# An attention block fused with a squared-ReLU feed-forward block: six early output tiles as half sums, and loads issued in other places

## The chip, the cores and the metric

The kernel runs on one core of one Trainium2 chip. A core has five engines with queues of their own: TensorE (PE in the profile; its weight loads are PEld), VectorE (DVE), ScalarE (ACT), GpSimd (POOL) and SyncE (SP), and 16 DMA engines that all queues share. The metric is device time in microseconds (us).

## The reference

Attention with a softmax that has one more term in its denominator, over 8 batches of 12 heads, 448 positions and 64 dimensions; its output, as 3584 tokens of 768, goes through two matrix products with a squared ReLU between them.

```python
scores = scale * np.matmul(q, k.transpose(0, 1, 3, 2))
m = np.max(scores, axis=-1, keepdims=True)
e = np.exp(scores - m)
attn = e / (np.sum(e, axis=-1, keepdims=True) + np.exp(-m) + 1e-09)
x = matmul(attn, v), heads side by side            # (3584, 768)
h = x @ w_in                                       # (3584, 2048)
g = np.maximum(h, 0.0) ** 2
out = g @ w_out                                    # (3584, 768), float32
```

The term exp(-m) beside the shifted sum is a 1 beside the unshifted one, so the kernel takes no maximum: it computes exp(scores), sums it, and takes exp(-ln(sum + 1)) as the reciprocal (both sides scaled by 1/256).

## The kernel before, in words

Everything on TensorE is float16 with float32 sums. Heads go in quads of four (`NQ` = 3 quads a batch), keys in chunks of 64 (`KC` = 7). The steps are written out by hand as short words in two strings, and one loop issues them in that order. `ORDER` (L662) covers batches 0 to 2; `CYCLE` (L719) is one period of the software pipeline and runs for batches 3 to 7, each time with that batch's scores, the feed-forward input of the batch before it and the output tiles before that. A tail (L754 to L762) ends the last batch. Every engine takes its instructions in the order of the string and waits for operands by semaphores; so a step that waits holds all later steps of its own engine, and of no other.

The words of `ORDER`, with the engine in brackets:

- `d`: start a load (POOL's DMA queue; the transposing loads and all stores are on SP). The numbers index `LOADS` (L614): 0 to 7 are q and k of one quad of batches 0 to 2, 8 to 13 are v of batches 0 and 1 by quad, 14 is v of batch 2, 15 to 18 are quarters of W_in ("chunks" below), 19 to 22 are quarters of W_out, 23 is `stage(3)`, 24 is `load_third`.
- `W` (PE): matmuls on a constant, to keep the array at work while the first loads come. `c` (ACT or DVE): casts of the first quad.
- `t`, `T` (PE): transposes of q and k into PSUM; `u`, `U` (DVE, or ACT where the last number is 1): their copies to SBUF.
- `s` (PE): scores into one of two double banks `sp`; `e` (ACT): the exponential, which frees that buffer. So a score waits for the exponential of the last but one score. Numbers 0 to 23 are pieces of batch 0, split in two halves of the queries, three quads, and four pieces each: 0 to 3 are quad 0 of the first half, 12 to 15 quad 0 of the second. Numbers from 24 are whole chunks of later quads.
- `p`, `v` (PE): exp(scores) times v. `b`, `a` (DVE): adding the exponentials over chunks; `y`, `S` (PE): the rest of that sum, by ones. `z`, `Z` (ACT): ln(sum + 1); `n`, `M` (ACT): the exponential of minus that; `x`, `X` (DVE): the product with the attention output, which gives `xt`.
- `i`, `j` (PE): `xt` times a block of W_in (`i` is half a batch, two blocks; `j` a whole batch, one block, in pieces). `r`, `k` (ACT or DVE): ReLU; `g`, `l` (DVE): its square, into `gs`.
- `o n,f0,f1` (PE): tile n of the output, 128 tokens by 384 columns, the products with blocks f0 to f1 of `gs`. `O n,act` (ACT or DVE): its way out of PSUM, and its store. `EARLY` = 6 such tiles lie in `ORDER`.
- `P`: PSUM changes hands. Up to there, results other than scores have two banks (`m_psum`) and a double bank; afterwards a ring of four banks (`ring`). A bank is used again by the fourth allocation after, once it has been emptied.

TensorE's 128x128 array can be used whole (128*128 in the profile), in two halves by columns (128*64) or in four quarters (64*64) that work side by side. Scores, products with v and sums use 64*64; transposes use 128*64; `i` and `j` of `ORDER` use 128*128, `j` of `CYCLE` 128*64. `out_piece` (L536) has both ways for output tiles: whole, with one bank; or with `rows` in quarters, where the two halves of the 128 hidden rows sum into two banks `op` and `lo`. In that case `out_first` (L553) takes the first bank out of PSUM, and `out_second` (L561) adds the second on DVE and stores. `ORDER` uses the whole form and `out_done`; `CYCLE` uses quarters and has the word `Q` for `out_second`.

From batch 3 on, q and k come through DRAM: `stage(b)` (POOL queue) writes them as float16, `transposed_loads(b)` (SP) reads them back transposed in three planes of the tile `qk`, `tail_keys(b)` (POOL) copies the last 64 keys of each head, and `load_v_quads(b)` (POOL queue) loads v. In `CYCLE` the word `d0`, near its end, issues all of this for the next batch, and `stage` for the one after.

Of the kernel before, what the change touches and what calls it, by code (L numbers as in the profile page):

```python
# [16 lines left out]
def kernel(  # L17
# [142 lines left out]
    def transposed_loads(b):  # L160
        qk = qks[b] = qk_pool.tile([128, 3, COLS], FP16, name="qk")
        for i, n, x, c in ((0, "q", FRONT, H * S // 2), (1, "k", FRONT, H * S // 2), (2, "k", 0, COLS)):
            nc.sync.dma_start(
                out=qk[:, i, 0:c],
                in_=stages[n, b][x:x + c * 2 * D].rearrange("(r c) -> r c", c=2 * D),
                transpose=True,
            )
# [3 lines left out]
    def tail_keys(b):

        km = kms[b] = flat.tile([128, H, 64], FP16, name="flatq")
        for r in range(2):
            for odd in range(2):
# [445 lines left out]
    def quad_visit(n):  # L621
# [33 lines left out]
        "O": lambda n, act: out_done(128 * (n // 2), HALF * (n % 2), HALF, act),
    }

    def other_ring():
# [8 lines left out]
        U1,0,1,0,7,0 e14 e15 s17 p14 b3,0 b3,1 e17 s18 i0,7 d17 d5 b3,2 e18 b3,3 p15 y3 z3 b4,0 r0,7,0 s21 s19 e21 T1,1,1 d4 n3 b4,1 i0,6 U1,1,1,0,7,0 s20 d15
        T1,1,0 x3 b4,2 e19 b4,3 d16 s23 p16 p17 p18 r0,6,0 U1,1,0,0,7,0 e20 b5,0 e23 s22 e22 b5,1 p19 y4 s26 z4 n4 i0,4 g0,7 x4 r0,4,0 s27 i0,5 g0,6 b5,2 e26
        s25 e27 T1,2,1 s28 e25 p20 p21 r0,5,0 p22 s24 g0,5 b5,3 e28 d11 T1,2,0 p23 e24 s29 y5 e29 U1,2,1,0,7,0 U1,2,0,0,7,0 T2,0,0 T2,0,1 U2,0,0,0,7,0 z5 g0,4
        d6 U2,0,1,0,7,0 s30 n5 s32 a0,0 e30 d13 i0,0 i0,1 s33 x5 e32 r0,0,0 g0,0 r0,1,0 s31 i1,0 d12 g0,1 e33 i0,3 r1,0,0 e31 r0,3,1 s35 d7 s36 e35 P0 e36  # L670
        i0,2 s34 e34 a0,1 a0,2 g1,0 v0,0 a0,3 S0 v0,1 v0,2 v0,3 v0,4 Z0 v0,5 v0,6 M0 r0,2,0 g0,3 g0,2 s37 i1,3 a1,0 a1,1 e37 X0 r1,3,0 a1,2 g1,3 i1,6 s39 s40
        a1,3 e39 i1,1 r1,1,0 r1,6,0 s43 T2,2,0 e40 d20 T2,2,1 g1,6 e43 s42 g1,1 e42 U2,2,0,0,7,0 s41 d19 i1,5 r1,5,0 e41 s38 e38 T2,1,0 T2,1,1 U2,2,1,0,7,0
        U2,1,0,0,7,1 S1 a2,0 Z1 s44 U2,1,1,0,7,0 i1,4 i1,2 a2,1 e44 r1,4,1 s45 a2,2 g1,5 a2,3 v1,0 v1,1 M1 v1,2 v1,3 v1,4 v1,5 v1,6 r1,2,1 v2,0 S2 v2,1 X1
        g1,4 e45 g1,2 v2,2 v2,3 v2,4 Z2 v2,5 v2,6 M2 s47 X2 s46 i1,7 j3,0,2 r1,7,0 o0,0,4 j3,2,4 j1,0,2 j3,4,6 k3,0 j12,0,2 o0,4,8 j1,2,4 o0,8,12 e46 e47
        o0,12,16 s50 d21 g1,7 s51 j12,2,4 j1,4,6 k1,0 j5,0,2 e51 e50 l3 j5,2,4 j5,4,6 d23 O0,1 k5,1 j12,4,6 l5 o1,0,4 s48 s49 j6,0,2 e49 l1 e48 d22 k12,1 l12
        o1,4,8 o1,8,12 o1,12,16 s53 s52 e52 e53 j6,2,4 j10,0,2 o5,0,4 j6,4,6 O1,1 s55 k6,0 s54 j10,2,4 o5,4,8 j0,0,2 e55 a3,0 j10,4,6 j8,0,2 o5,8,12 j0,2,4
        a3,1 k10,1 o5,12,16 e54 s61 s57 l6 a4,0 j14,0,2 O5,0 e57 j14,2,4 j14,4,6 e61 j8,2,4 a3,2 j9,0,2 j9,2,4 j0,4,6 j9,4,6 a3,3 j8,4,6 l10 s56 k0,0 k14,0
        e56 l0 k8,1 s58 o2,0,4 o2,4,8 l14 d14 s59 v4,0 v4,1 v4,2 v4,3 a4,1 v4,4 v4,5 e58 k9,0 s60 e59 s64 o2,8,12 d24 l9 o2,12,16 a4,2 a4,3 j7,0,2 e60 v4,6
# [39 lines left out]

    CYCLE = """  # L719
# [5 lines left out]
        e3,1 o4,2,4 o6,14,16 s3,2 e3,3 o4,4,6 O6,1 a2,2 o4,6,8 s3,5 a2,3 o4,8,10 Q6 o4,10,12 e3,2 e3,5 o4,12,14 o4,14,16 O4,1 Q4 a3,0 s3,6 v2,0 v2,1  # L725
        S2 Z2 v2,2 v2,3 v2,4 v2,5 M2 v2,6 e3,6 X2 j2,0,2 j2,2,4 j2,4,6 k2,0 j13,0,2 j13,2,4 l2 j13,4,6 j3,0,2 k13,1 l13 j3,2,4 j15,0,2 j12,0,2 j15,2,4
        j0,0,2 j3,4,6 a3,1 j15,4,6 k3,1 a3,2 k15,1 j12,2,4 a3,3 l15 j0,2,4 j0,4,6 l3 j12,4,6 j10,0,2 j10,2,4 j4,0,2 k0,0 l0 k12,1 l12 j10,4,6 j6,0,2
        j7,0,2 j7,2,4 j7,4,6 j4,2,4 k10,0 j6,2,4 j4,4,6 l10 j6,4,6 k7,1 j5,0,2 l7 j5,2,4 k4,1 j11,0,2 k6,0 j11,2,4 j11,4,6 j9,0,2 l6 j5,4,6 l4 j9,2,4
# [62 lines left out]
```

## Time and profile before

| | us |
|---|---|
| median of 3 runs | 397.14 (396.34 to 397.28) |
| profiled execution | 396.87 |
| its span | 394.8 |
| PE busy | 385.5 (98%) |
| DVE busy | 240.5 (61%) |
| ACT busy | 238.1 (60%) |
| POOL busy | 59.8 (15%) |

The span is the time from the first to the last instruction; the rest of the execution's time lies around it. Matmuls are pipelined, so the busy time of PE includes their overlap; how fast PE gets on is read from the distance between starts. A row of instructions gives its count after x, then busy us and the mean ns of one, then the idle time of its engine before it and what ended it. The first cycle starts with the first product of values that reads the tile `nn`, at 105.9 us, and the next ones at 151.1, 197.5, 242.8, 288.0; the tail follows at 333.2.

### The profile page before, as it was taken

The page shows a single profiled execution, that of the slowest core. Times are in us where ns is not written, and L with a number is a line of the kernel's source. Part 1 is how long each engine was busy: PE and PEld are TensorE (multiplying, and loading weights), DVE is VectorE, ACT ScalarE, POOL GpSimd, SP SyncE. Part 2 cuts the span into 40 slices and gives each one's busy share as a digit, 9 for nine tenths or more (in the row PEclk, how much of TensorE's full clock was granted, in tenths as well). Part 3 has the DMA queues.
Part 4 walks back from the last instruction along what each step waited for, and adds up shares of the span by engine and source line. Part 5 has one row for each costly group of instructions (what it writes and reads, how often), then busy time and mean ns, then how long its engine had stood idle before and what let it go on. Part 6 is the DMA issues. An engine that isn't in the chain of part 4 may idle for free.

```text
span 394.8 us, 13877 instructions
## 1 busy us (share of the span) xinstructions
PE 385.5 (98%) x6252; PEld 262.9 (67%) x6252; DVE 240.5 (61%) x445; ACT 238.1 (60%) x324; POOL 59.8 (15%) x96
## 2 busy tenths in 40 slices
PE   8789999999999999999999999999999999999997
PEld 4567776445599766896579866776677765555665
DVE  3889994385746765668536876567646785285000
ACT  4999895768479625895279834896269934100111
POOL 8354500003200032000500016000500000000000
PEclk9999999999999999999999999999999999999999
DMA  8999999568942579419692398527652100100222
GB/s 146 203 204 206 203 206 208 98 127 154 191 85 63 113 140 181 96 43 161 113 203 75 77 193 127 129 64 141 126 74 68 58 7 2 62 0 14 68 80 81
DMA packets 75051, 45.33 MB, mean 115 GB/s; under 512 B 47472, under 2 KB 72944, under 8 KB 74992
## 3 DMA queue, kind: packets, MB, share of 16 engines
q0 software_dynamic: 24752, 22.62, 36.3%
q1 hardware_dynamic: 49952, 21.59, 25.0%
q8 instruction: 49, 0.80, 0.8%
q10 hardware_dynamic: 288, 0.23, 0.2%
q14 instruction: 10, 0.08, 0.1%
HBM read 45.69 MB, written 17.93 MB: 161 GB/s over the span
## 4 chain that ended last, share of the span: by engine, by line
PE 94%; DVE 3%; ACT 1%; issue 1%; DVEq 0%; ACTq 0%
PE mp L92 81%; PE sp L92 9%; PE xp L92 2%; PE mp L198 2%; ACT et L245 1%; DVE qk L208 1%; DVE half L334 1%; DVE half L332 0%; PE mp L225 0%; ACT rcp L356 0%; ACT rcp L363 0%; DVE qk L235 0%; DVE half L338 0%; DVE half L336 0%; DVE rt L496 0%
## 5 line engine op out<-in xcount | busy, mean ns | idle before, releaser
L92 PE MATMUL mp<-wout,gs 64*64 64x384 f16 (+2 forms) x2592 | 166.7, 322 | 0.0
L92 PE MATMUL mp<-xt,win 128*64 128x448 f16 (+2 forms) x1344 | 151.4, 339 | 0.1
L245 ACT ACTIVATE et<-sp 128x896 f16<-128x896 f32 (+1 forms) x131 | 110.8, 889 | 30.1 <-PE sp L92 28.9
L92 PEld LDWEIGHTS <-win 128*64 128x64 f16 (+1 forms) x1344 | 89.6, 106 | 58.7 <-issue 7.4
L92 PEld LDWEIGHTS <-gs 64*64 64x64 f16 (+1 forms) x2592 | 105.9, 106 | 34.3 <-issue 1.1
L494 ACT ACTIVATE rt<-mp 128x448 f16<-128x448 f32 x55 | 29.3, 544 | 57.2 <-PE mp L92 52.4
L500 DVE TENSOR_TENSOR gs<-rt 128x448 f16<-128x448 f16 x128 | 49.2, 401 | 22.2 <-ACT rt L494 19.8
L92 PE MATMUL sp<-qk 64*64 64x224 f16 (+1 forms) x1056 | 57.4, 274 | 2.5 <-issue 0.9
L496 DVE TENSOR_SCALAR rt<-mp 128x448 f16<-128x448 f32 x73 | 45.2, 621 | 23.0 <-PE mp L92 21.5
L557 ACT ACTIVATE ot<-mp 128x384 f32<-128x384 f32 (+2 forms) x34 | 16.4, 481 | 51.3 <-PE mp L92 50.8
L92 PEld LDWEIGHTS <-qk 64*64 64x64 f16 x1056 | 36.1, 114 | 14.4 <-issue 7.4
L179 POOL COPY flatq<-qk 64x384 f16<-64x384 f16 x20 | 12.4, 643 | 205.9 <-DMA qk<-stage_k 205.6
L245 ACT ACTIVATE nn<-sp 128x896 f16<-128x896 f32 x42 | 36.7, 915 | 1.9 <-PE sp L92 1.8
L478 DVE TENSOR_TENSOR xt<-mp,rcp 128x448 f16<-128x448 f32 x42 | 24.3, 620 | 20.0 <-ACT rcp L457 17.8
...
L563 DVE SCALAR_TENSOR_TENSOR ot<-mp,ot 128x384 f32<-128x384 f32 x35 | 19.5, 556 | 16.9 <-ACT ot L557 15.3
L454 ACT ACTIVATE rcp<-sp,one_b 128x896 f32<-128x896 f32 x21 | 21.2, 1007 | 10.0 <-PE sp L92 10.0
L92 PE MATMUL mp<-et,vn 64*64 64x448 f16 (+1 forms) x448 | 25.1, 343 | 0.0
L559 DVE TENSOR_SCALAR ot<-mp 128x384 f32<-128x384 f32 x23 | 12.8, 556 | 19.6 <-PE mp L92 19.5
L432 DVE TENSOR_TENSOR half<-et 128x1792 f16<-128x1792 f16 x15 | 16.3, 1087 | 7.0 <-ACT et L245 6.9
L457 ACT ACTIVATE rcp<-rcp 128x896 f32<-128x896 f32 x21 | 20.0, 952 | 0.6
L434 DVE TENSOR_TENSOR half<-half,et 128x1792 f16<-128x1792 f16 x15 | 16.4, 1091 | 0.7 <-ACT et L245 0.3
...
## 6 DMA issues: line engine op xcount, KB each, us to landing
...
vn<-in_v_dram POOLq DMA_DIRECT2D x10, 288.0 KB, 4.8
...
```

The source lines that it names most:

```text
L92: return nc.tensor.matmul(out_, lhsT, rhs, start=start, stop=stop)
L245: nc.scalar.activation(out=out_, in_=in_, func=AF.Exp, scale=scale)
L432: nc.vector.tensor_add(esq[m], a[:, 0:w], a[:, w:2 * w])
L434: nc.vector.tensor_add(esq[m], esq[m], z[:, 0:w])
L454: nc.scalar.activation(out=rcp, in_=zp[:, :, 0:S], func=AF.Ln, bias=one_b)
L457: nc.scalar.activation(out=zqs[m], in_=zqs[m], func=AF.Exp, scale=-1.0)
L478: nc.vector.tensor_mul(xts[b][:, 2 * g + i, :], xqs[m][i][:, 0:S], zqs[m][:, i, :])
L494: nc.scalar.activation(out=rt[:, 0:m], in_=hp[:, 0:m], func=AF.Relu)
L496: nc.vector.tensor_scalar(out=rt[:, 0:m], in0=hp[:, 0:m], scalar1=0.0, scalar2=None, op0=ALU.max)
L500: nc.vector.tensor_mul(gs[:, f0:f0 + per, t0 % RING:t0 % RING + n], r, r)
L557: nc.scalar.activation(out=ot, in_=op[:, 0:w], func=AF.Copy, scale=OUT_SCALE)
L563: nc.vector.scalar_tensor_tensor(out=ot, in0=lo[:, 0:w], scalar=OUT_SCALE, in1=ot, op0=ALU.mult, op1=ALU.add)
```

## The change

The early tiles go in quarters with two banks, as in `CYCLE`, and `ORDER` gets the word `Q`. `ORDER` is written anew: the same scores, products and loads in another sequence, with some copies on the other engine. In `CYCLE`, `d0` is cut into seven words: `d0` to `d2` are one transposing load each, `d3` and `d4` the copies of the last keys by plane, `d5` the loads of v, `d6` the staging of the batch after. The first three stand after `Q5`, the others after `Q4`, with `d6` ahead of `d5`.

```diff
-    def transposed_loads(b):
-        qk = qks[b] = qk_pool.tile([128, 3, COLS], FP16, name="qk")
-        for i, n, x, c in ((0, "q", FRONT, H * S // 2), (1, "k", FRONT, H * S // 2), (2, "k", 0, COLS)):
-            nc.sync.dma_start(
+    PLANES = (("q", FRONT, H * S // 2), ("k", FRONT, H * S // 2), ("k", 0, COLS))
+
+    def transposed_load(b, i):
+        qk = qk_of(b)
+        n, x, c = PLANES[i]
+        nc.sync.dma_start(
...
-        "o": lambda n, f0, f1: out_piece(128 * (n // 2), HALF * (n % 2), HALF, range(f0, f1)),
-        "O": lambda n, act: out_done(128 * (n // 2), HALF * (n % 2), HALF, act),
+        "o": lambda n, f0, f1: out_piece(128 * (n // 2), HALF * (n % 2), HALF, range(f0, f1), True),
+        "O": lambda n, act: out_first(128 * (n // 2), HALF * (n % 2), HALF, act),
+        "Q": lambda n: out_second(128 * (n // 2), HALF * (n % 2), HALF),
...
-        d0 W8 c1,4,0 c0,0,1 c1,0,1 t0,0,0 c0,4,1 t1,0,0 u0,0,0,0 t1,0,4 u1,0,0,0 t0,0,4 u1,0,4,0 s0 d8 d1 u0,0,4,0 t0,1,0 e0 t1,1,0 u0,1,0,0 u1,1,0,0 s1 s2 e1
-        d10 t0,1,4 u0,1,4,0 t1,1,4 u1,1,4,1 T0,1,0 T0,1,1 s3 U0,1,0,0,4,0 e2 U0,1,1,0,4,0 s4 U0,1,0,4,7,1 e3 d9 U0,1,1,4,7,0 d2 p0 e4 p2 s16 p1 e16 b0,0 b0,1
...
+        d0 c1,4,0 c0,0,1 c1,0,1 c0,4,1 W8 t0,0,0 t1,0,0 u0,0,0,1 t1,0,4 u1,0,0,0 u1,0,4,0 t0,0,4 s0 t0,1,0 u0,0,4,1 e0 u0,1,0,0 t1,1,0 u1,1,0,0 s1
+        t0,1,4 t1,1,4 u0,1,4,0 e1 u1,1,4,0 s2 s12 T0,1,0 T0,1,1 U0,1,0,0,4,0 e2 U0,1,1,0,4,0 U0,1,1,4,7,0 s3 e12 e3 U0,1,0,4,7,0 b0,0 d1 s4 T0,2,0 e4
+        s6 U0,2,0,0,4,0 d8 T0,2,1 b0,1 U0,2,1,0,4,0 e6 s5 s9 d2 b0,2 d9 p0 e5 b0,3 p2 d10 b1,0 s8 U0,2,1,4,7,0 p1 p3 y0 U0,2,0,4,7,0 e9 s15 e8 e15 d4
...
+        s19 p15 y3 s23 e19 z3 e23 n3 s20 x3 i0,6 e20 s21 p16 s22 p17 b4,3 p18 U1,2,1,0,7,0 d15 e21 p19 r0,6,0 y4 b5,0 i0,7 e22 z4 b5,1 s29 r0,7,0 s28
+        T1,1,1 d6 n4 x4 e29 e28 T1,1,0 p20 p21 b5,2 b5,3 U1,1,1,0,7,0 p22 p23 g0,6 y5 z5 n5 s27 s25 e27 U1,1,0,0,7,0 e25 i0,4 g0,7 x5 i1,7 s26 e26 s24
...
+        g0,0 S2 o0,0,4 g1,2 o0,4,8 o0,8,12 s49 Z2 o0,12,16 M2 X2 O0,0 s46 d21 Q0 j0,0,2 j0,2,4 e49 e46 j2,0,2 j0,4,6 j2,2,4 j2,4,6 k0,1 s51 o2,0,4 s53
+        e51 o2,4,8 s45 o2,8,12 e53 d14 k2,0 s48 o2,12,16 e45 O2,0 d24 e48 s54 l0 Q2 j15,0,2 j15,2,4 l2 j12,0,2 j15,4,6 j5,0,2 k15,0 l15 j5,2,4 j12,2,4
...
-        def following():
+        def following(n):
             if b + 1 < B:
-                transposed_loads(b + 1)
-                tail_keys(b + 1)
-                load_v_quads(b + 1)
-                if b + 2 < B:
+                if n < 3:
+                    transposed_load(b + 1, n)
+                elif n < 5:
+                    tail_keys(b + 1, (n - 2,))
+                elif n == 5:
+                    load_v_quads(b + 1)
+                elif b + 2 < B:
                     stage(b + 2)
...
-        v1,2 v1,3 M1 v1,4 O5,0 v1,5 Q5 v1,6 X1 o6,0,2 s3,4 e3,4 o6,2,4 s3,0 e3,0 o6,4,6 o6,6,8 a2,0 o6,8,10 o6,10,12 s3,1 o4,0,2 o6,12,14 a2,1 s3,3
+        v1,2 v1,3 M1 v1,4 O5,0 v1,5 Q5 d0 d1 d2 v1,6 X1 o6,0,2 s3,4 e3,4 o6,2,4 s3,0 e3,0 o6,4,6 o6,6,8 a2,0 o6,8,10 o6,10,12 s3,1 o4,0,2 o6,12,14
...
+        a2,1 s3,3 e3,1 o4,2,4 o6,14,16 s3,2 e3,3 o4,4,6 O6,1 a2,2 o4,6,8 s3,5 a2,3 o4,8,10 Q6 o4,10,12 e3,2 e3,5 o4,12,14 o4,14,16 O4,1 Q4 d3 d4 d6 d5
...
-        j8,0,2 j8,2,4 k5,1 j9,4,6 l5 j1,0,2 k11,0 j8,4,6 j1,2,4 j1,4,6 k9,1 j14,0,2 j14,2,4 l11 l9 k8,0 j14,4,6 l8 k1,1 l1 k14,0 S3 Z3 d0 l14 M3
+        k14,0 S3 Z3 l14 M3
```

More of the change, by code (lines that the diff above doesn't have):

```diff
@@ L158, in stage, with tail_keys @@
                                     in_=src[0:lo + TOTAL - hi].rearrange("(r w) -> r w", r=1))
-    def transposed_loads(b):
-        qk = qks[b] = qk_pool.tile([128, 3, COLS], FP16, name="qk")
-        for i, n, x, c in ((0, "q", FRONT, H * S // 2), (1, "k", FRONT, H * S // 2), (2, "k", 0, COLS)):
-            nc.sync.dma_start(
[L164 to L167, printed above, removed]
-    kms = {}
[L171 to L175, printed above, removed]
+    PLANES = (("q", FRONT, H * S // 2), ("k", FRONT, H * S // 2), ("k", 0, COLS))
[3 more added lines that the diff above has]
+        nc.sync.dma_start(
+            out=qk[:, i, 0:c],
+            in_=stages[n, b][x:x + c * 2 * D].rearrange("(r c) -> r c", c=2 * D),
+            transpose=True,
+        )
+    def transposed_loads(b):
+        for i in range(3):
+            transposed_load(b, i)
+    kms = {}
+    def tail_keys(b, planes=(1, 2)):
+        if b not in kms:
+            kms[b] = flat.tile([128, H, 64], FP16, name="flatq")
+        km = kms[b]
+        for which in planes:
+            for r in range(2):
                 rows_ = slice(64 * r, 64 * r + 64)
-                which, x = (1, 0) if odd == r else (2, odd)
+                odd, x = (r, 0) if which == 1 else (1 - r, 1 - r)
                 src = qks[b][rows_, which, x:x + H * S // 2].rearrange("p (h x) -> p h x", h=H)
@@ L667 @@
[L667 to L678, printed above, removed]
@@ L679 @@
-        e64 S4 Z4 M4 O2,0 S3 j7,2,4 o4,0,4 l8 o4,4,8 o4,8,12 o4,12,16 j7,4,6 Z3 s62 X4 s63 M3 O4,0 v3,0 v3,1 v3,2 v3,3 v3,4 v3,5 e62 v3,6 s65 X3 k7,1 j4,0,2
-        e65 o3,0,4 a5,0 o3,4,8 o3,8,12 o3,12,16 j15,0,2 j4,2,4 j4,4,6 l7 e63 j15,2,4 a5,1 j2,0,2 O3,1 a5,2 j2,2,4 a5,3 j15,4,6 k4,0 j13,0,2 j11,0,2 S5 Z5
-        k15,0 M5 l4 l15 j2,4,6 k2,0 j13,2,4 l2 j11,2,4 j13,4,6 j11,4,6 k11,1 k13,1 l11 l13
+        d0 c1,4,0 c0,0,1 c1,0,1 c0,4,1 W8 t0,0,0 t1,0,0 u0,0,0,1 t1,0,4 u1,0,0,0 u1,0,4,0 t0,0,4 s0 t0,1,0 u0,0,4,1 e0 u0,1,0,0 t1,1,0 u1,1,0,0 s1
@@ new lines @@
+        t0,1,4 t1,1,4 u0,1,4,0 e1 u1,1,4,0 s2 s12 T0,1,0 T0,1,1 U0,1,0,0,4,0 e2 U0,1,1,0,4,0 U0,1,1,4,7,0 s3 e12 e3 U0,1,0,4,7,0 b0,0 d1 s4 T0,2,0 e4
+        s6 U0,2,0,0,4,0 d8 T0,2,1 b0,1 U0,2,1,0,4,0 e6 s5 s9 d2 b0,2 d9 p0 e5 b0,3 p2 d10 b1,0 s8 U0,2,1,4,7,0 p1 p3 y0 U0,2,0,4,7,0 e9 s15 e8 e15 d4
+        s7 z0 s10 e7 T1,0,1 b1,1 b1,2 b2,0 U1,0,1,0,7,0 d18 T1,0,0 e10 n0 s11 U1,0,0,0,7,0 s13 p4 x0 e11 b2,1 s14 p5 p6 b1,3 d3 e13 b2,2 p8 e14 p7 y1
+        d13 p9 p10 p11 b2,3 y2 z1 s17 b3,0 d17 z2 b3,1 b3,2 s16 n1 n2 x1 T1,2,0 T1,2,1 e17 x2 e16 s18 p12 p13 U1,2,0,0,7,0 e18 b3,3 b4,0 b4,1 b4,2 p14
@@ new lines @@
+        s19 p15 y3 s23 e19 z3 e23 n3 s20 x3 i0,6 e20 s21 p16 s22 p17 b4,3 p18 U1,2,1,0,7,0 d15 e21 p19 r0,6,0 y4 b5,0 i0,7 e22 z4 b5,1 s29 r0,7,0 s28
+        T1,1,1 d6 n4 x4 e29 e28 T1,1,0 p20 p21 b5,2 b5,3 U1,1,1,0,7,0 p22 p23 g0,6 y5 z5 n5 s27 s25 e27 U1,1,0,0,7,0 e25 i0,4 g0,7 x5 i1,7 s26 e26 s24
+        r0,4,0 i1,5 g0,4 r1,7,0 r1,5,0 g1,7 P0 e24 a0,0 s30 a0,1 s32 e30 e32 g1,5 i1,6 s33 s34 i0,1 r1,6,0 e33 e34 s36 e36 r0,1,0 a0,2 a0,3 d11 i1,0
+        s37 s31 e37 v0,0 v0,1 e31 v0,2 v0,3 v0,4 v0,5 g1,6 d16 S0 Z0 d5 v0,6 d7 d19 i1,1 r1,0,0 M0 g0,1 i1,3 g1,0 s35 r1,3,1 e35 r1,1,0 s40 X0 e40
@@ new lines @@
+        T2,1,1 U2,1,1,0,7,0 T2,1,0 U2,1,0,0,7,1 T2,0,0 T2,0,1 U2,0,1,0,7,1 a1,0 s43 g1,3 s39 e43 U2,0,0,0,7,0 a1,1 g1,1 i1,4 i0,3 r1,4,1 a1,2 e39 d12
+        a1,3 g1,4 i0,5 s41 S1 r0,5,0 r0,3,0 T2,2,0 T2,2,1 e41 g0,5 v1,0 Z1 s38 v1,1 v1,2 e38 v1,3 v1,4 M1 v1,5 v1,6 U2,2,0,0,7,0 s42 s44 U2,2,1,0,7,0
+        i0,2 i0,0 e42 r0,2,1 a2,0 X1 i1,2 g0,3 d20 e44 s50 r1,2,1 s47 v2,0 v2,1 a2,1 v2,2 v2,3 g0,2 d23 e50 d22 v2,4 v2,5 a2,2 e47 r0,0,0 a2,3 v2,6
+        g0,0 S2 o0,0,4 g1,2 o0,4,8 o0,8,12 s49 Z2 o0,12,16 M2 X2 O0,0 s46 d21 Q0 j0,0,2 j0,2,4 e49 e46 j2,0,2 j0,4,6 j2,2,4 j2,4,6 k0,1 s51 o2,0,4 s53
@@ new lines @@
+        e51 o2,4,8 s45 o2,8,12 e53 d14 k2,0 s48 o2,12,16 e45 O2,0 d24 e48 s54 l0 Q2 j15,0,2 j15,2,4 l2 j12,0,2 j15,4,6 j5,0,2 k15,0 l15 j5,2,4 j12,2,4
+        j12,4,6 j11,0,2 j5,4,6 k5,1 j13,0,2 e54 a3,0 k12,0 j13,2,4 j11,2,4 j11,4,6 a3,1 j13,4,6 a3,2 s55 s52 e55 e52 l12 l5 o3,0,4 o3,4,8 s57 k13,0
+        o3,8,12 k11,0 s56 o3,12,16 O3,0 e57 a4,0 Q3 s60 o1,0,4 e56 s58 a3,3 e60 a4,1 o1,4,8 e58 s61 e61 o1,8,12 o1,12,16 S3 O1,0 Z3 v3,0 v3,1 v3,2
+        v3,3 v3,4 v3,5 M3 Q1 v3,6 X3 s63 s65 a4,2 o5,0,4 o5,4,8 e63 o5,8,12 e65 s59 o5,12,16 s62 e59 e62 v4,0 O5,1 a4,3 v4,1 v4,2 v4,3 S4 Z4 v4,4 v4,5
@@ L682 @@
+        v4,6 M4 s64 Q5 l13 j4,0,2 l11 j4,2,4 j9,0,2 j9,2,4 j9,4,6 X4 j4,4,6 j8,0,2 j8,2,4 j1,0,2 k4,0 l4 k9,0 l9 j6,0,2 j1,2,4 j8,4,6 k8,0 e64 j1,4,6
+        j6,2,4 k1,1 j14,0,2 j14,2,4 l8 j6,4,6 k6,0 j3,0,2 l6 l1 a5,0 j7,0,2 j3,2,4 a5,1 j3,4,6 j14,4,6 k3,1 k14,1 j7,2,4 a5,2 j7,4,6 l3 j10,0,2
+        j10,2,4 j10,4,6 k10,1 o4,0,4 o4,4,8 l14 o4,8,12 o4,12,16 k7,1 a5,3 S5 O4,1 Z5 l7 l10 Q4 M5
     """
@@ L715, in cycle @@
             "Q": lambda n: out_second(128 * ((first + n) // 2), HALF * ((first + n) % 2), HALF),
-            "d": lambda n: following(),
+            "d": lambda n: following(n),
         }
@@ L723 @@
         o3,12,14 o3,14,16 a1,3 s2,4 o5,0,2 e2,4 o5,2,4 o5,4,6 o5,6,8 s2,5 O3,0 s2,1 o5,8,10 o5,10,12 o5,12,14 o5,14,16 e2,5 e2,1 Q3 S1 v1,0 v1,1 Z1
-        v1,2 v1,3 M1 v1,4 O5,0 v1,5 Q5 v1,6 X1 o6,0,2 s3,4 e3,4 o6,2,4 s3,0 e3,0 o6,4,6 o6,6,8 a2,0 o6,8,10 o6,10,12 s3,1 o4,0,2 o6,12,14 a2,1 s3,3
[L725 to L728, printed above, removed]
-        j8,0,2 j8,2,4 k5,1 j9,4,6 l5 j1,0,2 k11,0 j8,4,6 j1,2,4 j1,4,6 k9,1 j14,0,2 j14,2,4 l11 l9 k8,0 j14,4,6 l8 k1,1 l1 k14,0 S3 Z3 d0 l14 M3
+        v1,2 v1,3 M1 v1,4 O5,0 v1,5 Q5 d0 d1 d2 v1,6 X1 o6,0,2 s3,4 e3,4 o6,2,4 s3,0 e3,0 o6,4,6 o6,6,8 a2,0 o6,8,10 o6,10,12 s3,1 o4,0,2 o6,12,14
+        a2,1 s3,3 e3,1 o4,2,4 o6,14,16 s3,2 e3,3 o4,4,6 O6,1 a2,2 o4,6,8 s3,5 a2,3 o4,8,10 Q6 o4,10,12 e3,2 e3,5 o4,12,14 o4,14,16 O4,1 Q4 d3 d4 d6 d5
+        a3,0 s3,6 v2,0 v2,1 S2 Z2 v2,2 v2,3 v2,4 v2,5 M2 v2,6 e3,6 X2 j2,0,2 j2,2,4 j2,4,6 k2,0 j13,0,2 j13,2,4 l2 j13,4,6 j3,0,2 k13,1 l13 j3,2,4
+        j15,0,2 j12,0,2 j15,2,4 j0,0,2 j3,4,6 a3,1 j15,4,6 k3,1 a3,2 k15,1 j12,2,4 a3,3 l15 j0,2,4 j0,4,6 l3 j12,4,6 j10,0,2 j10,2,4 j4,0,2 k0,0 l0
+        k12,1 l12 j10,4,6 j6,0,2 j7,0,2 j7,2,4 j7,4,6 j4,2,4 k10,0 j6,2,4 j4,4,6 l10 j6,4,6 k7,1 j5,0,2 l7 j5,2,4 k4,1 j11,0,2 k6,0 j11,2,4 j11,4,6
+        j9,0,2 l6 j5,4,6 l4 j9,2,4 j8,0,2 j8,2,4 k5,1 j9,4,6 l5 j1,0,2 k11,0 j8,4,6 j1,2,4 j1,4,6 k9,1 j14,0,2 j14,2,4 l11 l9 k8,0 j14,4,6 l8 k1,1 l1
+        k14,0 S3 Z3 l14 M3
     """
```

2 lines of the change are left out of this document (removed).

## The prediction

> **What bounds the kernel now.** I read the page from the top: busy shares, the slices, then the chain that ended last.
>
> ```profile
> PE 385.5 (98%) x6252; PEld 262.9 (67%) x6252; DVE 240.5 (61%) x445; ACT 238.1 (60%) x324; POOL 59.8 (15%) x96
> ...
> PE   8789999999999999999999999999999999999997
> ...
> PE 94%; DVE 3%; ACT 1%; issue 1%; DVEq 0%; ACTq 0%
> ```
>
> TensorE (PE) carries 94% of the chain; what is not PE lies in the first slices. So three things can shorten the run: less PE work, fewer gaps between PE instructions, less waiting at the start. Busy time can't show the second, because matmuls overlap. I took it from the starts in the timeline, around the end of the hand-written order.
>
> ```profile
> 100.10 3.57 PE L92 MATMUL mp<-xt,win 128*128 128x448 f16 x18
> 103.60 0.38 PE L92 MATMUL sp<-half,ones 64*64 64x448 f16 x4
> 103.91 2.07 PE L92 MATMUL mp<-xt,win 128*128 128x448 f16 x10
> 105.91 1.52 PE L92 MATMUL mp<-nn,vn 64*64 64x448 f16 x28
> ...
> 107.45 2.77 PE L92 MATMUL mp<-wout,gs 64*64 64x384 f16 x64
> 110.05 0.36 PE L92 MATMUL sp<-qk 64*64 64x224 f16 x8
> ```
>
> Inside one array form the starts are even. The 64 small output matmuls take 110.05 - 107.45 = 2.60 us, 0.1625 us per four. Forty-eight full output matmuls from 334.59 to the next instruction at 342.40 take 7.81 us, 0.1627 each. A full matmul of 448 columns takes 0.189. Where the form changes, time is lost: 18 x 0.189 = 3.40 after 100.10 is 103.50, but the next start is 103.60; the four 448-column sums (one pass, 0.189) end at 103.79, the next start is 103.91; ten more end at 105.80, the next start is 105.91. Leaving the full form costs 0.102 us, entering it from 64x64 costs 0.126; between 64x64 and 128x64 it is 0.120 and 0.124 by the same reckoning.
>
> Then the stages.
>
> ```profile
> 0.00:4.28 4.28, 3.50 (x9) 1.02 (x9) 0.31 (x4) 2.03 (x4) 3.13 (x9) 1.00 0.62 136
> 4.28:24.70 20.42, 15.93 (x386) 11.76 (x386) 15.05 (x36) 17.42 (x30) 11.84 (x18) 1.00 1.20 190
> 24.70:62.00 37.30, 36.99 (x617) 28.28 (x618) 34.31 (x65) 33.89 (x45) 13.27 (x19) 1.00 1.26 206
> 62.00:105.90 43.90, 43.90 (x344) 22.34 (x344) 25.64 (x46) 26.88 (x35) 6.08 (x10) 1.00 0.84 147
> 105.90:151.10 45.20, 45.20 (x905) 34.77 (x908) 29.39 (x53) 29.06 (x40) 6.04 (x10) 1.00 0.59 110
> 151.10:197.50 46.40, 45.52 (x912) 34.73 (x908) 29.35 (x53) 29.86 (x39) 5.73 (x10) 1.00 0.67 119
> ```
>
> Columns: length, then busy time of PE, PEld, DVE, ACT, POOL, granted clock, DMA share, GB/s. Only 4.28 to 24.7 us has real PE idleness; there ACT has no gap from 9.11 to 26 us. From 24.7 on PE starves nowhere, apart from one 1.1 us hole at 162.4 (in the second cycle of 46.4 us instead of 45.2), which the waits put down to
>
> ```profile
> PE sp L92 <- issue: 0.9, 1, 0.9
> ```
>
> that is, to nothing that the program waits for.
>
> **The change, part by part.** The sum is made against the profiled execution: 396.87 us, a span of 394.8 and 2.07 around it; the median of the runs shown is 0.27 above it.
>
> *Six tiles as half sums.* Each trades 16 full matmuls (16 x 0.1627 = 2.60) for 64 small ones (16 x 0.1625 = 2.60): PE work is unchanged. The 48 more matmuls and weight loads per tile are no cost by the 107.45 row, which has the same mix. Each tile needs a second bank and one more eviction on DVE (the row of line 563, 556 ns): 6 x 0.556 = 3.3 us on an engine busy 25.6 of 43.9 us from 62 to 105.9.
>
> *Form changes.* Output steps now share the form of scores, values and sums. I counted steps in the two orders. 64x64 to full: 21, now 13. Full to 64x64: 22 (one where the order meets the first cycle), now 13. 64x64 to 128x64: 11, now 10; full to 128x64 1 and 1; 128x64 to full 1, now 0; 128x64 to 64x64 11 and 11. Saved: 8 x 0.126 + 9 x 0.102 + 0.124 + 0.122 = 2.17 us. These lie on PE between 30 and 106 us, where PE is the chain, so all of it counts.
>
> *The start.* PE is saturated only once W_in products exist, and the first one stands behind a score that waits for ACT. Before: `i0,7` starts at 24.69, behind s18, which needs the buffer that e15 frees. After: `i0,6`, behind s20, which needs e19. In the new order the copy u1,1,4 (L233, 0.49 us on ACT, ahead of e2 with 0.49 us of idleness before it) goes to DVE, so e2 can start near 8.95 instead of 9.62. From e2 to e19 ACT then holds 13 full exponentials at 0.80 (start to start when ACT is full), e3 at 0.66, four short ones at 0.43, two Ln at 0.60 and one at 0.68, three reciprocals at 0.47: 10.40 + 0.66 + 1.72 + 1.88 + 1.41 = 16.07. With 0.2 for s5, now behind T0,2,1, whose keys land near 12.1: e19 ends near 25.2 and `i0,6` starts near 25.7. Its PE work ahead is 17.6 us, against 15.5 ahead of `i0,7` (stream time of the steps plus form changes). So PE has lost 8.1 us by then instead of 9.15. Later losses: before, 0.4 (33.8, 43.85, among others); after, 0.3 for s22 and s25, which meet e20 and e28 within 0.1 to 0.3 us. Total 8.4 against 9.57 (105.91 less 96.34 of PE work): 1.2 us gained. Bounds: nothing gained if DVE rather than ACT leads (it has 15.05 of 20.42 us, and needs b1,3 and b2,3 before z1 and z2), 2.2 if no small wait comes. I take 1.2, from the ACT rows, as ACT is the engine without gaps.
>
> The other copies that change engine (u0,0,0 and u0,0,4 to ACT, U0,1,0,4,7 back to DVE) run where ACT idles 2.34 us before e0, and on DVE ahead of b0,0, which needs e2 only. Nothing is taken for them.
>
> *Order of the loads.* One queue from POOL delivers about 205 GB/s until 73 us, so what stands earlier lands earlier. By its landings (1.15 us per q, k or v piece, 1.9 per half of a W_in chunk) I estimate for the new order: v of group 0 near 13.3 (first product 13.6), W_in chunk 3 at 24.6 (`i0,6` 25.7), chunk 2 at 31.7 (`i0,4` 32.3), v of batch 1 group 1 at 52.1 (v1 53.7), W_out at 51 to 56 and 66 to 70 (o0 61, o3 76). All in time, two by 0.6 us or less; I take nothing and keep 2 us as a loss. load_third moves up: its three transposes hold SP some 8 us ahead of store Q2; there are four output buffers, so no eviction waits.
>
> *Loads in the cycles.* In batches 3 to 6 the three transposes (3.2, 2.6 and 3.6 us on SP at 133.4) go ahead of the stores Q6 and Q4, which so leave up to 9 us late; their buffers are wanted again in the next cycle, over 20 us later. The four POOL copies (643 ns) follow the transposes. On POOL the stage transfers (landing 12.7 us after issue at 149.5) now precede the v loads (some 5 us): about 137.5 + 12.7 + 5 = 155 by the old cycle's clock, against a first use near 168. Cover 13 us: nothing. The stage transfers no longer lie beside the next cycle's small matmuls, where the 1.1 us hole stood (the second stage transfer landed at 162.2). I keep the hole in the sum, for want of proof.
>
> Sum: 396.87 - 2.17 - 1.2 = 393.5; I say 393.4 for a small chance that the hole goes (then 392.4).
>
> **The rivals.**
>
> *Only the form changes pay* (DVE's half sums lead at the start): 396.87 - 2.17 = 394.7. For it: PE waits for DVE's half sums at 13.3 (0.44) and 18.25 (0.69) and for x1 at 22.92 (0.88).
>
> *A load comes late*: `i0,4` or p0 waits up to 2 us with all of PE behind it: 395.4 to 396.7. For it: margins under 0.7 us. Against: PE has no DMA wait at all in the old trace.
>
> *Banks bound the output tiles, and the kernel is slower.* After the change of pools there are four banks. An output tile takes two, held until O (491 to 556 ns) and Q (556) are done, with about 0.25 us of hand-over. If the next user stood right behind, each tile would cost 0.25 + 0.49 + 0.56 = 1.3 us, six tiles 7.8 us: 401.3. It decides from 0.57 us a tile, where 3.4 us are eaten. Against: counted in PE work, the step that takes a bank again stands 1.1 to 4.5 us behind its last matmul, in the old order 1.4 to 5.5 with no stall. The Trainium skill, "TensorEngine Tiling (Array Packing)", PSUM Bottleneck and Gotcha 1: PSUM Pressure, warns that tiling does not speed up emptying PSUM and spreads row tiles over more banks. By that rule the time would come out in this rival's range; the cycles of this trace, which run such tiles on four banks without a gap, speak against it.
>
> *Instruction supply fails beside the transposes*: holes like 162.4, now in the small-matmul phase where the transposes run, twice in each of four cycles at 1.1 us: 393.5 + 7.7 = 401.2. It decides from four holes. One hole in four such stretches speaks for it weakly.
>
> **How the numbers follow.** Forecast 0.50 (own range 392.2 to 394.4), form changes alone 0.20, late load 0.11, banks 0.12, supply 0.07. A measurement can tell 0.3%, 1.2 us. Faster: 0.50 + 0.20 + half of the late loads = 0.76; same 0.05; slower 0.19. The range runs from 391.8 (forecast without the hole, and half a microsecond more) to 397.0, which leaves out the two slower cases.
>
> **What would show it.** The first cycle (first `mp<-nn,vn`) starts near 102.6 instead of 105.91; cycles stay at 45.2 us; the first W_in product starts near 25.7. Forms change as counted and the output groups of 64 keep 2.60 us. Wrong would be PE waiting on DVE or ACT at output tiles after 60 us, on DMA at 13 or 32 us, or holes beside transposes.

## The result and the profile after

The changed kernel takes 393.34 us (median of 6 runs, 392.84 to 394.58) against 397.08 (6 runs, 396.09 to 397.31): a ratio of 0.9916, with a 95% interval of 0.9896 to 0.9937. The forecast was 393.4. The profiled execution took 393.45 us, its span 391.7, 3.1 us less than the old span of 394.8. The busy shares and slices of the page of the changed kernel, beside those of before:

```profile
PE 383.6 (98%) x6540; PEld 255.8 (65%) x6540; DVE 243.8 (62%) x450; ACT 238.7 (61%) x325; POOL 60.8 (16%) x96
...
PE   8889999999999999999999999999999999999996
...
PE 91%; ACT 5%; DMA 2%; DVE 1%; issue 1%; POOL 1%; POOLq 0%; ACTq 0%; DVEq 0%
```

There are 288 more matmuls (6 x 48), as the six tiles make them, yet PE is busy for less. In the chain ACT has gone from 1% to 5%, and DMA is new with 2%; they come back below. The windows of the changed kernel, cut at its own stages (length, then PE, PEld, DVE, ACT, POOL busy, clock, DMA share, GB/s):

```profile
4.28:25.70 21.42, 17.97 (x438) 12.76 (x437) 16.90 (x41) 19.95 (x35) 13.15 (x20) 1.00 1.22 191
25.70:62.00 36.30, 35.98 (x580) 27.96 (x580) 31.49 (x60) 32.09 (x43) 11.95 (x17) 1.00 1.24 207
62.00:103.56 41.56, 41.51 (x628) 25.12 (x623) 28.75 (x53) 25.99 (x34) 6.58 (x10) 1.00 1.05 175
103.56:148.73 45.17, 45.17 (x908) 30.89 (x904) 29.35 (x52) 30.18 (x40) 6.36 (x10) 1.00 0.70 129
148.73:193.90 45.17, 45.17 (x908) 30.88 (x904) 30.05 (x53) 29.80 (x39) 6.22 (x10) 1.00 0.64 116
```

The first row ends with the first W_in product, the third with the first cycle; all five cycles take 45.17 us. In the old profile the cycles took, by the same cuts:

```profile
105.91:151.14 45.23, 45.23 (x905) 34.77 (x908) 29.43 (x53) 29.05 (x40) 6.04 (x10) 1.00 0.59 110
151.14:197.48 46.34, 45.46 (x908) 34.71 (x904) 29.29 (x53) 29.86 (x39) 5.71 (x10) 1.00 0.67 119
197.48:242.82 45.34, 45.34 (x908) 33.70 (x904) 29.46 (x53) 29.85 (x39) 7.84 (x14) 1.00 0.68 129
```

The two cycles left out take 45.17 each. So the 3.1 us divide thus. The first W_in product starts 1.07 us later (25.69 against 24.62), with about 2.1 us more PE work ahead of it. From there to the first cycle it is 77.87 us against 81.28, 3.41 less. The five cycles together take 225.85 against 227.25, 1.40 less. The tail, from 329.41 and from 333.16, is 0.61 longer; its last matmul starts 58.58 us into the tail in both traces, so those 0.6 us lie behind the last matmul.

The total agrees with the forecast, the division doesn't: `ORDER` saved 2.35 us (103.56 against 105.91) where 3.4 had been forecast, and the cycles saved 1.40 where nothing had been put in the sum. The experiments are about both.

Below, "the way" is the distance from the first W_in product to the first cycle, and "the start" is when that product begins.

### The profile page after: what moved, and what is told of

The parts are those of the page before. It is cut to its first block, busy times and chain, and to the rows that moved or that the text cites. A ratio compares the mean times of both kernels' runs of the same rounds, so it can differ in the third digit from the quotient of the medians.

```text
span 391.7 us, 14476 instructions
## 1 busy us (share of the span) xinstructions
PE 383.6 (98%) x6540; PEld 255.8 (65%) x6540; DVE 243.8 (62%) x450; ACT 238.7 (61%) x325; POOL 60.8 (16%) x96
## 4 chain that ended last, share of the span: by engine, by line
PE 91%; ACT 5%; DMA 2%; DVE 1%; issue 1%; POOL 1%; POOLq 0%; ACTq 0%; DVEq 0%
PE mp L92 80%; PE sp L92 8%; ACT et L253 3%; DMA nn<-in_k_dram 2%; PE mp L206 1%; PE xp L92 1%; ACT rcp L371 0%; ACT rcp L364 0%; DVE half L442 0%; DVE ot L567 0%; DVE half L446 0%; DVE ot L571 0%; POOL nn L116 0%; DVE xt L379 0%; POOL flatk L129 0%
## 5 line engine op out<-in xcount | busy, mean ns | idle before, releaser
L92 PE MATMUL mp<-xt,win 128*64 128x448 f16 (+2 forms) x1344 | 149.0, 339 | 0.0
L92 PEld LDWEIGHTS <-gs 64*64 64x64 f16 (+1 forms) x2880 | 99.6, 106 | 37.1 <-issue 1.2
L253 ACT ACTIVATE et<-sp 128x896 f16<-128x896 f32 (+2 forms) x131 | 110.4, 894 | 17.7 <-PE sp L92 17.1
L92 PE MATMUL sp<-qk 64*64 64x224 f16 (+1 forms) x1056 | 54.6, 273 | 2.0 <-ACT et L253 1.3
L504 DVE TENSOR_SCALAR rt<-mp 128x448 f16<-128x448 f32 x72 | 44.4, 621 | 17.3 <-PE mp L92 15.6
L187 POOL COPY flatq<-qk 64x384 f16<-64x384 f16 x20 | 13.5, 675 | 189.6 <-DMA qk<-stage_k 189.1
L92 PEld LDWEIGHTS <-qk 64*64 64x64 f16 x1056 | 32.2, 114 | 15.2 <-issue 5.9
L571 DVE SCALAR_TENSOR_TENSOR ot<-mp,ot 128x384 f32<-128x384 f32 x41 | 22.8, 556 | 19.9 <-ACT ot L565 12.2
L92 PEld LDWEIGHTS <-vn 64*64 64x64 f16 x756 | 22.0, 107 | 9.5 <-issue 0.3
L567 DVE TENSOR_SCALAR ot<-mp 128x384 f32<-128x384 f32 x24 | 13.3, 555 | 21.5 <-PE mp L92 21.4
```

The costliest lines, as they stand in the source:

```text
L92: return nc.tensor.matmul(out_, lhsT, rhs, start=start, stop=stop)
L253: nc.scalar.activation(out=out_, in_=in_, func=AF.Exp, scale=scale)
L504: nc.vector.tensor_scalar(out=rt[:, 0:m], in0=hp[:, 0:m], scalar1=0.0, scalar2=None, op0=ALU.max)
L571: nc.vector.scalar_tensor_tensor(out=ot, in0=lo[:, 0:w], scalar=OUT_SCALE, in1=ot, op0=ALU.mult, op1=ALU.add)
```

## The experiments

The kernels below ran in three groups, each with the old kernel on the same chip, where its median was 396.44 to 396.55 us and not 397.08. The ratios are to these, and they compare better than times across groups do.

### The load words of the cycles alone, and the rest alone

The first kernel has the old `ORDER` and whole tiles, with the new `CYCLE`; the second has everything but the new `CYCLE`.

```diff
 first:  ORDER, "o", "O" of the old kernel
 second: CYCLE and following() of the old kernel
```

> The old order and whole tiles in batches 0 to 2, the new load words in the cycles. Theory A (the 1.1 us hole at 162.4 of the old trace comes from staging transfers beside the next cycle's small matmuls, which the new words move away): the first cycle starts at 105.9 as before, all cycles take 45.17 us, the time is 1.1 to 1.4 us under the old one, 395.5 to 396. Rival (the hole falls at random, whatever the loads): no difference in the median, 396.3 to 397.3, with a hole in some runs.

Measured: 395.63 us (12 runs), ratio 0.9983 (0.9968 to 0.9998) to the old kernel, 0.9 us in the medians. First cycle at 106.01, cycles of 45.33, 45.19, 45.31, 45.17, 45.17, together 226.17 against 227.25. No hole over 0.12 us, but not quite even. The time is in the range of theory A, the gain a little under its 1.1 to 1.4 us. Which of the moved words removed the hole, this run doesn't tell.

> The new order and quarter tiles in batches 0 to 2, the old d0 in the cycles. Theory A: the first cycle starts at 103.6 as in the changed kernel, cycles are 45.17 to 46.3 with one hole or more, the time is 394.4 to 394.8. Rival (hole at random): 393.3, as the changed kernel.

Measured: 393.63 us (6 runs, 393.01 to 394.58), ratio 0.9927 (0.9910 to 0.9944). First cycle at 103.84, cycles of 45.17, 46.39, 45.17, 45.44, 45.17. The profile has a hole of the old kind, with no releaser, in the same cycle:

```profile
157.66 0.49 PE L92 MATMUL mp<-wout,gs 64*64 64x384 f16 x7
159.06 0.32 PE L92 MATMUL mp<-wout,gs 64*64 64x384 f16 x1 [0.91 <-issue]
```

The staging transfer of k that was under way landed at 159.9. This profile is of the slowest of the six runs, and the median lies under the 394.4 of theory A, nearer to the rival. So the two parts of the change are nearly independent: the order gives about 3, the load words about 1. The times of the second kernel spread over both theories' values, and its ratio's interval overlaps with the changed kernel's, so the size of the second part rests on the first kernel and on the profiles.

### Whole tiles in the new order, quarter tiles in the old one

```diff
 third: the new kernel with whole tiles
-        "o": lambda n, f0, f1: out_piece(..., range(f0, f1), True),
-        "O": lambda n, act: out_first(...),
-        "Q": lambda n: out_second(...),
+        "o": lambda n, f0, f1: out_piece(..., range(f0, f1)),
+        "O": lambda n, act: out_done(...),
+        "Q": lambda n: None,
 fourth: the old kernel with quarter tiles, and in ORDER
-   ... O0,1 ...
+   ... O0,1 Q0 ...
```

> The new kernel with its six early tiles whole again (one bank each, Q does nothing), in the new order. Form changes between 64x64 and full rise from 13 and 13 to 27 and 27, which is 14 x 0.126 + 14 x 0.102 = 3.19 us more. Theory (form changes are what the half sums are worth): first cycle at 106.4 to 106.8, time 396.2 to 396.6; up to 0.4 us less if the bank wait at 85.6 goes as well. Rival (the new sequence, not the form, brings the gain): first cycle near 103.6, time 393.3.

Measured: 396.40 us (10 runs), first cycle at 106.32, just under what was expected. The way is 81.05 us against 77.87: 3.18 more, where 28 more form changes at the two prices of the old trace make 3.19. That the two agree to 0.01 is luck: the waits for banks, 0.39 us in the changed kernel, are gone, but a score at 27.7 now waits 0.29, which it doesn't there. The prices hold to about 0.1 us. The form changes thus carry the whole gain that `ORDER` has: with whole tiles in it, the new order is no faster than the old kernel (ratio 0.9997, 0.9984 to 1.0010), though this kernel has the new `CYCLE` as well.

> The old kernel with its six early tiles as half sums (Q right behind O) in the old order. Form changes between 64x64 and full rise from 21 and 22 to 27 and 28: 6 x 0.126 + 6 x 0.102 = 1.37 us more, since those tiles lie among whole-array products there. Theory: first cycle at 107.3 plus what two banks a tile cost, time 398.2 to 400. Rival (the half sums pay by themselves): 395 or less.

Measured: 408.97 us (4 runs), ratio 1.032 (1.030 to 1.034); first cycle at 115.98, the way 91.95 us against 81.28, 10.7 more. This is far over the 398.2 to 400 that was expected. Form changes are 1.37 of the 10.7, which leaves some 9.3 for waiting for banks, the rival that had 0.12. The largest waits of PE in this kernel (what waited, for what; us in total, times, longest; all that end with an eviction on the way make 7.1, and the modelled ends of matmuls hide a part of each), and two places of its timeline:

```profile
PE mp L92 <- DVE rt L496: 2.1, 3, 0.7
PE mp L92 <- DVE xt L478: 1.8, 1, 1.8
PE mp L92 <- ACT ot L557: 1.4, 1, 1.4
PE mp L92 <- DVE ot L559: 0.9, 2, 0.6
```

```profile
76.89 0.93 PE L92 MATMUL mp<-xt,win 128*128 128x448 f16 x4
79.17 0.32 PE L92 MATMUL mp<-wout,gs 64*64 64x384 f16 x1 [1.35 <-ACT ot L557]
79.76 0.84 PE L92 MATMUL mp<-wout,gs 64*64 64x384 f16 x15 [0.28 <-DVE ot L563]
...
99.40 0.35 PE L92 MATMUL mp<-wout,gs 64*64 64x384 f16 x1
101.55 2.76 PE L92 MATMUL mp<-wout,gs 64*64 64x384 f16 x61 [1.80 <-DVE xt L478]
```

An output tile begins, finds its second bank still held by the tile before (until `Q`, L563) or by values (until `x`, L478), and all of PE stands behind it. Each tile holds two of four banks among W_in products that hold the others. The old trace's slack of 1.4 to 5.5 us was slack for one bank a tile.

### The 0.33 us at 85.6, and where load_third goes

In the changed kernel `o5` waits 0.33 us for its second bank, the one that `Q1` frees. DVE there:

```profile
81.87 0.55 DVE L571 SCALAR_TENSOR_TENSOR ot<-mp,ot 128x384 f32<-128x384 f32 x1
82.33 0.72 DVE L446 TENSOR_TENSOR half<-half,et 128x896 f16<-128x896 f16 x1
82.98 1.45 DVE L442 TENSOR_TENSOR half<-half,et 128x1792 f16<-128x1792 f16 x1
84.35 0.54 DVE L567 TENSOR_SCALAR ot<-mp 128x384 f32<-128x384 f32 x1
85.00 0.56 DVE L571 SCALAR_TENSOR_TENSOR ot<-mp,ot 128x384 f32<-128x384 f32 x1
```

The sum of line 442 takes 1.45 us, elsewhere 1.08, and that of line 446 0.72 instead of 0.62, while POOL copies the last keys. In the cycles too, the few sums over their usual 0.62 (0.87 at 135.1 and 136.0, 0.98 at 271.1) lie beside such copies:

```profile
82.02 1.51 POOL L187 COPY flatq<-qk 64x384 f16<-64x384 f16 x2 [33.16 <-DMA qk<-stage_k]
84.12 1.47 POOL L187 COPY flatq<-qk 64x384 f16<-64x384 f16 x2 [0.58 <-DMA qk<-stage_k]
```

```diff
-   ... O2,0 d24 e48 ...   ... Q5 l13 ...
+   ... O2,0 e48 ...       ... Q5 d24 l13 ...
```

> The new kernel with load_third (d24) moved from behind O2 to behind Q5, one place later than the last early tile but one. Theory (the POOL copies that follow the transposes, at 82.0 to 85.6, stretch DVE's sums, so that O1 and Q1 come late and o5 waits 0.33 us for its second bank): the hole at 85.6 and the 0.06 at 90.4 go, the first cycle starts 0.3 to 0.5 us earlier, at 103.1 to 103.3, time 392.8 to 393.1. Rival (the order of DVE's own steps makes O1 late): the hole stays, 393.3.

Measured: the way is 77.49 us, 0.38 less, and the holes at 85.6 and 90.4 are gone, as expected. But the time is 395.03 us (10 runs), ratio 0.9971 (0.9955 to 0.9987) against the new kernel's 0.9916, where 392.8 to 393.1 had been expected: the first cycle takes 47.49 us. What load_third starts in turn, the v loads and the staging of batch 4, now runs beside the small matmuls of that cycle:

```profile
105.10 2.65 POOL L110 DMA_DIRECT2D vn<-in_v_dram  x4
107.71 0.61 POOL L154 DMA_DIRECT2D stage_q<-in_q_dram  x1
108.28 0.61 POOL L154 DMA_DIRECT2D stage_k<-in_k_dram  x1
```

```profile
113.55 0.25 PE L92 MATMUL sp<-qk,flatq 64*64 64x224 f16 x1 [0.48 <-issue]
...
119.74 0.32 PE L92 MATMUL mp<-wout,gs 64*64 64x384 f16 x1 [1.34 <-issue]
```

The transfers issued there landed from 110.4 to 120.8. This speaks for theory A better than the runs meant for it: holes without a releaser appear in another cycle as soon as these transfers are moved there. The trace's records of instruction transfers (queue 8, one to every 4.3 to 4.8 us of small matmuls in the changed kernel: 108.2, 112.5, 117.0, 121.8) have late ones ahead of the holes: 102.9, 111.1, 117.5 here; 148.1, 156.6 in the kernel with the old `CYCLE`, ahead of its hole at 159.06. That PE runs out of instructions whose delivery waits among the data transfers fits this; it was not shown by itself, and in the old trace a distance of 6.9 us (198.2 to 205.0) came with a hole of 0.14 us only.

### One copy back on ACT

```diff
-   e1 u1,1,4,0 s2 s12
+   e1 u1,1,4,1 s2 s12
```

> The new kernel with the one copy u1,1,4 on ACT again. Theory (ACT's chain sets the start): e2 starts 0.5 to 0.7 us later, the first W_in product at 26.1 to 26.4 instead of 25.69, the first cycle up to that much later, 104.0 to 104.2, time 393.8 to 394. Rival (DVE's half sums set it): the freed DVE brings the first product earlier or leaves it at 25.7, time 393.3 or less.

Measured: 393.03 us (4 runs, 392.62 to 393.39), first W_in product at 25.57, first cycle at 103.43. The price set on the copy is wrong: e2 starts 0.15 us later and not 0.5 to 0.7, and nothing is lost. ACT in the changed kernel, then in this one:

```profile
8.82 1.73 ACT L253 ACTIVATE et<-sp 128x896 f16<-128x896 f32 x2 [0.29 <-PE sp L92]
10.72 1.60 ACT L253 ACTIVATE et<-sp 128x448 f16<-128x448 f32 x3 [0.18 <-PE sp L92]
```

```profile
8.46 0.49 ACT L241 ACTIVATE qk<-mp 64x384 f16<-64x384 f16 x1
8.97 3.24 ACT L253 ACTIVATE et<-sp 128x896 f16<-128x896 f32 x5
```

With the copy on DVE, e2 starts at 8.82, and e3 still only at 10.72, because its score stands behind the transpose of quad 1's keys. With the copy on ACT, e2 starts at 8.97 and ACT runs through to the same point. The chain of the changed kernel names what it waits for: the keys' landing at 9.64, and from there ACT.

```profile
3.58 6.06 DMA nn<-in_k_dram
9.64 0.04 issue
9.69 0.58 PE mp L206 x14
10.27 0.22 PE xp L92
10.49 0.21 PE sp L92 x5
10.70 0.02 issue
10.72 2.42 ACT et L253 x4
```

The numbers of this run are those of the rival, but its cause isn't seen: no work of DVE lies on the changed kernel's chain between the landing and the first product, and the keys landed 0.11 us earlier in the run with the copy on ACT. That ACT sets the pace doesn't fall with the copy. With the copy on ACT, ACT has no idle time from e2 to the first product, 16.60 us. The kernel with whole tiles, whose keys landed at 8.87, has the copy on DVE and no idle time on ACT either, from e2 at 8.68 to the product at 25.27, 16.59 us:

```profile
8.68 6.90 ACT L253 ACTIVATE et<-sp 128x896 f16<-128x896 f32 x10 [0.29 <-PE sp L92]
```

In the changed kernel the same distance is 16.87, so the keys' landing adds 0.27 us to ACT's chain.

### Three waits taken away at once

```diff
-   ... O2,0 d24 e48 ...  ... Q5 l13 ...      -   z3 e23 n3 s20      -   a0,1 s32 e30 e32 g1,5 i1,6 s33
+   ... O2,0 e48 ...      ... Q5 d24 l13 ...  +   z3 n3 e23 s20      +   a0,1 i1,6 s32 e30 e32 g1,5 s33
```

> The new kernel with three waits taken away by order: load_third late as in the run above; n3 ahead of e23, so that x3 frees the double bank that p16 waits for at 27.45 (0.29); s32 behind i1,6, so that it no longer waits 0.26 for e24 at 37.2. Theory (after 25.7 us PE is the chain, so each wait on PE counts in full): the first cycle starts 0.8 to 1.0 us earlier, at 102.5 to 102.8, time 392.3 to 392.6. Rival (the waits move on to the next step): 393 to 393.3.

Measured: 396.65 us (12 runs), no better than the old kernel (ratio 1.0003, 0.9986 to 1.0020). The way is 78.80 us, 0.9 longer: with s32 later, PE waits 0.6 at 38.3 and 1.0 at 40.9. The rival is right, and worse than stated. The first cycle takes 47.41 us, with a hole of 1.8 us at 121.0, as in the kernel with load_third late (a staging transfer landed at 121.5).

### More transfers in the cycles

```diff
+    def more_traffic(b):
+        for n, t in (("q", q), ("k", k)):
+            more = nc.dram_tensor(f"more_{n}{b}", (TOTAL,), FP16, kind="Internal").ap()
...
+        more_traffic(b)
```

> The new kernel with two more staging transfers per cycle into tensors that nobody reads, issued behind the cycle's other loads, so that some 11 us of transfers run beside the first part of the next cycle, where the small matmuls are. It computes the same. Theory A (holes without a releaser come from transfers beside the small matmuls): cycles show holes of 0.2 to 1.2 us again, some longer than 45.3; time 394 to 396.5. Rival (holes at random): cycles 45.17, time 393.3.

Measured: 394.68 us (10 runs); cycles of 45.17, 45.60, 45.19, 45.34, 45.17, 0.63 together above the even ones. There are holes again, 0.44 us at 159.2 and 0.18 at 253.7, but in the first and third cycles the added transfers ran beside the small matmuls too (landing at 107.4 and 110.8, 202.6 and 205.8) and cost no more than 0.02. So such transfers can make a hole and need not. And the cycles are the smaller part: in this profile the first W_in product starts at 27.00 with the same `ORDER`, 1.31 us later than in the changed kernel's.

### What sets the start

In the profiles with the new start of `ORDER` I compared the first W_in product with the landings of the first loads. In six of the seven so far it starts 16.05 us after the keys of quad 1 (9.64 in the changed kernel's trace, so 25.69) or 11.93 us after v of quad 0 (14.15 in the kernel with the old `CYCLE`: 26.08), whichever is later. The seventh, of the kernel with whole tiles, doesn't fit: its landings (8.87 and 12.45) would give 24.92, and the product starts at 25.27. There ACT's chain is the later term, 16.6 us from e2, as said above. With this third term all seven come out to 0.02 us, a fit made after the fact.

```diff
-   d9 p0 e5 b0,3 p2 d10 b1,0 s8 U0,2,1,4,7,0 p1 p3 y0 U0,2,0,4,7,0 e9 s15 e8 e15 d4
+   d9 e5 b0,3 d10 b1,0 s8 U0,2,1,4,7,0 U0,2,0,4,7,0 e9 s15 p0 p2 p1 p3 y0 e8 e15 d4
```

> The new kernel with the first products of values p0 to p3 and y0 moved behind s15, so that a late landing of v of group 0 no longer holds the scores. Theory B (the new start hangs on landings: in the six profiles of this order the first W_in product starts 16.05 us after the landing of the keys of quad 1, or 11.93 us after that of v of group 0, whichever is later): the first product starts 16.0 to 16.1 us after the keys' landing even where v lands after 14 us; time as the new kernel's or up to 0.6 us less. Rival (landings do not matter, the start varies by itself): no such relation; time as the new kernel's.

Measured: keys landed at 10.72, v at 14.06, first product at 26.83 (keys + 16.11); 393.83 us (6 runs). The keys were the later term here anyway, so this profile says nothing on v.

```diff
-   s58 a3,3 e60 a4,1 o1,4,8 ...  M3 Q1 v3,6
+   s58 a3,3 e60 o1,4,8 ...       M3 Q1 a4,1 v3,6
```

> As the run above, and the DVE sum a4,1 moved behind Q1, so that O1 and Q1 no longer stand behind it while the POOL copies stretch it. Theory (DVE's queue is late there, the bank is not the cause by itself): the hole of 0.33 us at 85.6 goes, the way from the first W_in product to the first cycle shrinks from 77.87 to 77.5 us, time 0.3 to 0.4 us under the run above. Rival (the wait moves to X3, v4 or j4): 77.8.

Measured: keys at 9.53, v at 14.40, first product at 25.64 (keys + 16.11), where the old place of p0 would have given 26.33: v no longer counts. The hole at 85.6 is gone and the way is 77.50 us, as expected; DVE empties the tile before it sums:

```profile
82.30 0.62 DVE L446 TENSOR_TENSOR half<-half,et 128x896 f16<-128x896 f16 x1
83.52 0.56 DVE L567 TENSOR_SCALAR ot<-mp 128x384 f32<-128x384 f32 x1 [0.61 <-PE mp L92]
84.18 0.56 DVE L571 SCALAR_TENSOR_TENSOR ot<-mp,ot 128x384 f32<-128x384 f32 x1
84.66 1.08 DVE L442 TENSOR_TENSOR half<-half,et 128x1792 f16<-128x1792 f16 x1
```

The time is 393.81 us (5 runs); the 0.3 to 0.4 us under the run above, which had been expected, don't show.

> The new kernel again, beside the two others on one chip. Theory B: the first W_in product again at the later of (keys of quad 1 landed + 16.05) and (v of group 0 landed + 11.93), within 0.15 us; 77.9 us from there to the first cycle; cycles 45.17; time 392.8 to 394.6 with the landings. Rival: another relation.

Measured: keys at 10.14, v at 13.54, first product at 26.19, as stated (10.14 + 16.05); the way 77.78; cycles of 45.17; 393.72 us (5 runs). The medians of these three kernels, on one chip, lie within 0.11 us of each other: 0.3 us of way can't be seen under a start that moves by 0.5 us between two profiles of the same kernel (25.69 and 26.19).

## Why the prediction was right, and where it was wrong

**Six tiles as half sums: right.** PE's work stayed the same. Nothing was lost to the 288 more matmuls.

**Form changes, 2.17 us: right.** The changed kernel with whole tiles confirms the two prices to about 0.1 us in 3.19. This is the whole net gain of `ORDER`: its 2.35 us are 2.17 and 0.18 that are left of the start.

**The start, 1.2 us: the term "later losses ... after, 0.3" failed, and so did a part of the reason.** "PE has lost 8.1 us by then" came out as forecast: 25.69, with 25.69 - 17.64 = 8.05 us lost, against 24.62 - 15.55 = 9.07 before (the prediction read 24.69 for 24.62). The later losses, by the same count of PE work, measured 1.34 us (77.87 less 76.53), against 0.48 before: p16 waits 0.3 for x3, s32 0.26 for e24, one transpose 0.2 at 47.25, a W_in product 0.14 at 34.2, o5 and j4 0.39 for banks. So 0.2 us were left of 1.2. Of the reason, "ACT is the engine without gaps" holds: the forecast had 16.75 us from e2 to the first product (8.95 to 25.7), and where ACT isn't idle it takes 16.6. That e2 starts earlier because a copy leaves ACT was disproved: with the copy back on ACT, e2 starts at 8.97 and not at the old kernel's 9.62, and the kernel is as fast. And the landing of quad 1's keys was left out, which holds ACT up by 0.27 us in the changed kernel, so that 25.69 met 25.7 partly by luck. "PE has no DMA wait at all in the old trace" was true of the old order alone.

**Order of the loads: landings right, consequence wrong.** v of group 0 landed at 13.07 (13.3 forecast), chunk 3 of W_in at 24.52 (24.6), chunk 2 at 31.79 (31.7). Putting the second quad ahead of v made v one of the two landings that can decide; over the profiles it landed between 12.45 and 15.07. Of the late-load rival the place p0 was right, with 0.3 to 0.8 us in three of the variants' profiles and nothing in the changed kernel's own.

**load_third: wrong in size.** SP was held from 67.76 to 82.14, 14.4 us and not 8. The first of the three took 7.6 of it, beside W_out and v transfers that landed at 70.6 and 75.4; that these were the cause was not tested. No output buffer stopped an eviction in `ORDER`, as said; but the POOL copies that follow stretched DVE's sums, and that cost 0.39 us on PE. The prediction had given the copies no price.

**Loads in the cycles: the mechanism was named, the size was set to nothing.** "I keep the hole in the sum, for want of proof": its removal brought 1.40 us in the profile of the changed kernel, and in the kernel with this part alone 1.08 in the profile and 0.9 in the medians. Why PE stops there stays open.

**The rivals.** Form changes alone (394.7) is nearly what `ORDER` did, and would have been the result without the cycles. Banks: no more than 0.39 us here, but in the old order more than the 7.8 that the rival named, some 9.3 us beside 1.37 of form changes. What the Trainium skill, "TensorEngine Tiling (Array Packing)", PSUM Bottleneck and Gotcha 1: PSUM Pressure, says (tiling does not speed up the emptying of PSUM, and row tiles take more banks) agrees with that run, by those 9.3 us, and with the changed kernel only in its 0.39 us. Holes beside the transposes: none; they came beside the staging transfers.

So 393.4 met 393.34 by luck: an excess of 1.0 us on `ORDER`, a lack of 1.4 on the cycles and 0.6 us more in the tail, which no term had, nearly cancelled.
